# Turning the column order of the matrix passes in five of eight feed-forward stages

## The chip, the core and the metric

The kernel runs on one core of one Trainium2 chip. The metric is the time of one execution on the device in microseconds (us), the median of the runs shown. The core's engines appear in the profile as PE (TensorE, the matrix engine), PEld (its weight loads, which overlap PE), DVE (VectorE), ACT (ScalarE), POOL (GpSimd) and SP (SyncE, which only issues transfers here).

## The reference

Attention with a sigmoid in place of the softmax, and behind it two feed-forward blocks (the first with a squared ReLU, the second with a gate):

```
scores = scale * np.matmul(q, k.transpose(0, 1, 3, 2)) - np.log(S)
attn = 1.0 / (1.0 + np.exp(-scores))
x = np.matmul(attn, v)                        # 4 batches, 12 heads, S = 448, 64 wide
x = x.transpose(0, 2, 1, 3).reshape(1792, 768)
h = x @ w_in;  r = np.maximum(h, 0.0);  x = (r * r) @ w_out          # 768 -> 2048 -> 768
h = x @ w_in2; x = (h * (1.0 / (1.0 + np.exp(-1.702 * h)))) @ w_out2
```

All data is float32.

## The kernel before, in words

The kernel has two parts. The first, up to about 128 us, is the attention: scores (lines 293, 298, 317), a sigmoid on ACT, and the product with the values (lines 332, 346). The second holds the two feed-forward blocks, and it is the part that the change touches.

Each feed-forward block has two products (into the 2048-wide layer and out of it), and each is done for one half of the batches at a time, so there are eight stages (`STAGES`, line 49). A stage multiplies a matrix cut into 2 by 2 quarters, by a scheme with seven products in place of eight: sums and differences of quarters are prepared on DVE and ACT, and the seven are called P1 to P7. `ORDER` says in which order a stage issues them, in 56 *units* (7 products by 8 slices, `NF = 8`). A unit is three pairs of a weight tile of 128 by 128 and an operand of 448 columns (`S = 448`, one batch row).

Float32 accuracy comes from splitting each number into a rounded part and a remainder, both in the type float32r. `plan_weights` makes the weight tiles: a load `ld` from the scratch memory, then ACT writes the rounded part into `s` (line 459) and DVE the remainder (line 461). `Operand` (line 401) does the same for the moving operand `t`: its index 0 is the rounded part and its index 1 the remainder. `product` (line 464) then issues three *passes* of TensorE for each pair, all into the same 448 columns of one PSUM bank:

```
o = mem["ps"][:, b, :S]
nc.tensor.matmul(o, sh[:, cols], t[:, 0, k], start=start, stop=False, skip_group_check=True)
nc.tensor.matmul(o, sh[:, cols], t[:, 1, k], start=False, stop=False, skip_group_check=True)
nc.tensor.matmul(o, lo[:, cols], t[:, 0, k], start=False, stop=stop, skip_group_check=True)
```

These are lines 475, 476 and 477 of the profile. So a unit has 9 passes, a stage 504, and the eight stages 4032. Each pass has a weight load of its own in the trace (PEld), and reads its 448 columns from left to right, one run of consecutive float32 numbers in SBUF, and writes one run of consecutive numbers in PSUM. The results leave PSUM through ACT and DVE (lines 153, 156 and 635; 153 and 156 are helpers through which most of their work is recorded).

The order of all instructions on all engines is fixed when the program is built, by a planner (`settle` and `run`) that works with its own table of costs; `UNIT_US` is its cost of a unit and does not depend on how a unit walks its columns.

Of the kernel before, what the change touches and what calls it, by code (L numbers as in the profile page):

```python
# [16 lines left out]
B, H, S, D = 4, 12, 448, 64  # L17
# [15 lines left out]
UNITS = 7 * NF  # L33
# [44 lines left out]
WINDOW, URGENT = 0.25, 3.0  # L78

PACE = (6, 6, 5, 1, 4, 5, 5)  # L80


@with_exitstack
def sigmoid_attention_two_ffn(ctx: ExitStack, tc: tile.TileContext, qk, v, w, outT):
# [3 lines left out]
    nc = tc.nc  # L88
# [28 lines left out]
    mem = {"ps": ppool.tile([P, 8, 512], F32, name="ps")}  # L117
# [346 lines left out]
    def product(unit, pairs, ready):  # L464
        sl = SL[unit // 2 % NSLOT]

        def go():
            sh, lo = sl[:, 0, unit % 2], sl[:, 1, unit % 2]
            if unit == 0:
                one = [nc.const_aps.tensor(1.0, [P, n], mybir.dt.bfloat16) for n in (P, D)]  # L470
                nc.tensor.matmul(mem["ps"][:, pairs[0][0], :D], *one, start=True, stop=True)  # L471
            for b, c, t, k, start, stop in pairs:
                cols = slice(c * P, (c + 1) * P)
                o = mem["ps"][:, b, :S]
                nc.tensor.matmul(o, sh[:, cols], t[:, 0, k], start=start, stop=False, skip_group_check=True)  # L475
                nc.tensor.matmul(o, sh[:, cols], t[:, 1, k], start=False, stop=False, skip_group_check=True)  # L476
                nc.tensor.matmul(o, lo[:, cols], t[:, 0, k], start=False, stop=stop, skip_group_check=True)  # L477

        units[unit].fn = go
        units[unit].need(lows[unit // 2], ready)  # L480
        for b in {b for b, *_ in pairs}:
            units[unit].need(*held.pop(b, ()))
# [181 lines left out]
    def settle():  # L664
# [16 lines left out]
        assert len(order) == len(Node.all)  # L681
        marks = [(0, 0.0), (PACE[0], pe_at[units[0]])]
        for st, count in enumerate(PACE[1:]):
            marks.append((marks[-1][0] + count, pe_at[units[(st + 1) * UNITS]]))
# [184 lines left out]
```

## Time and profile before

| what | value |
|---|---|
| median of 3 runs | 951.23 us (950.59 to 951.44) |
| the profiled execution | 950.77 us, of which the span in the trace 949.0 us |
| granted TensorE clock over the span | 1.000 |
| busy: PE, PEld, DVE, ACT, POOL | 944.6, 822.8, 809.3, 604.6, 53.5 us |
| instructions of PE | 4949 matmuls, 4949 weight loads |
| passes of the eight stages | 3 lines of 1344 each |

The span runs from the first to the last instruction; the 1.8 us between it and the execution's own time lie outside. Busy time of PE is no measure by itself, since a matmul in the trace lasts longer than the distance to the next one (they are pipelined): where passes matter, the distance between their starts is to be read.

### The profile page before, as it was taken

Reading aid. Unit: us, or ns where it says so; the run is one execution under the profiler, and the core shown is the slowest. Engines: PE = TensorE matmul, PEld = TensorE weight load, DVE = VectorE, ACT = ScalarE, POOL = GpSimd, SP = SyncE. Lnnn points to the kernel's source line nnn. Section 1 sums busy time; section 2 is a strip of 40 time slices with the busy share of each in tenths; the row PEclk is TensorE's granted clock in tenths of the full one; section 3 lists DMA queues with packets and bytes.
Section 4 is the critical chain, followed back from the end, with each engine's and each line's share of the span. In section 5 each row is a group of like instructions: output and inputs, shape, how many; then the busy total and the mean of one; then the engine's idle time right before and its main releaser. Section 6 shows DMA issues by size and latency. Waiting matters only on the chain.

```text
span 949.0 us, 13696 instructions
## 1 busy us (share of the span) xinstructions
PE 944.6 (100%) x4949; PEld 822.8 (87%) x4949; DVE 809.3 (85%) x839; ACT 604.6 (64%) x715; POOL 53.5 (6%) x100
## 2 busy tenths in 40 slices
PE   9999999999999999999999999999999999999998
PEld 4555479999999999999999999999999999999997
DVE  3989986699877999999999987999989999778662
ACT  6788776778868775555464666657684646445551
POOL 0110100000000000000000000000000000000000
PEclk9999999999999999999999999999999999999999
DMA  8899989999886766896567699877975448754341
GB/s 340 301 335 356 335 293 332 324 354 334 290 324 227 250 231 212 317 364 216 161 243 286 202 359 325 312 247 251 351 279 171 133 146 288 261 166 132 115 137 58
DMA packets 98627, 245.75 MB, mean 259 GB/s; under 512 B 10752, under 2 KB 72960, under 8 KB 94464
## 3 DMA queue, kind: packets, MB, share of 16 engines
q1 hardware_dynamic: 84736, 150.51, 46.5%
q0 software_dynamic: 13824, 94.38, 27.2%
q8 instruction: 38, 0.62, 0.3%
q14 instruction: 29, 0.24, 0.1%
HBM read 175.11 MB, written 69.73 MB: 258 GB/s over the span
## 4 chain that ended last, share of the span: by engine, by line
PE 100%; ACT 0%; issue 0%
PE ps L475 29%; PE ps L476 29%; PE ps L477 29%; PE ps L332 6%; PE ps L298 5%; PE ps L346 1%; PE ps L317 1%; PE ps L790 0%; PE ps L293 0%; ACT xq L635 0%; PE ps L471 0%
## 5 line engine op out<-in xcount | busy, mean ns | idle before, releaser
L475 PE MATMUL ps<-t,s 128*128 128x448 f32 x1344 | 490.9, 365 | 0.0
L477 PE MATMUL ps<-t,s 128*128 128x448 f32 x1344 | 490.8, 365 | 0.0
L476 PE MATMUL ps<-t,s 128*128 128x448 f32 x1344 | 490.8, 365 | 0.0
L153 ACT ACTIVATE s<-ld 128x768 fp32r<-128x768 f32 x224 | 189.4, 846 | 249.4 <-PE ps L476 206.6
L477 PEld LDWEIGHTS ps<-t,s 128*128 128x128 f32 x1344 | 252.5, 188 | 19.9
L476 PEld LDWEIGHTS ps<-t,s 128*128 128x128 f32 x1344 | 252.5, 188 | 19.9
L475 PEld LDWEIGHTS ps<-t,s 128*128 128x128 f32 x1344 | 252.5, 188 | 19.9
L156 DVE TENSOR_TENSOR s<-ld,s 128x768 fp32r<-128x768 f32 x224 | 213.6, 954 | 61.7 <-ACT s L153 56.6
L156 DVE TENSOR_TENSOR t<-h,t 128x1344 fp32r<-128x1344 f32 (+1 forms) x72 | 100.4, 1397 | 8.8 <-ACT t L153 8.7
L153 ACT ACTIVATE t<-h 128x1344 fp32r<-128x1344 f32 (+1 forms) x72 | 85.6, 1190 | 4.4 <-DVE h L156 2.9
L153 ACT ACTIVATE h<-ps 128x448 f32<-128x448 f32 x112 | 59.8, 536 | 27.0 <-PE ps L477 26.8
L153 ACT ACTIVATE a<-ps,bias 128x896 f32<-128x896 f32 x72 | 66.1, 1023 | 3.2 <-PE ps L293 3.2
L332 PE MATMUL ps<-a,rv 128*64 128x448 f32 x288 | 56.8, 543 | 0.1
L217 DVE SCALAR_TENSOR_TENSOR dec<-raw,dec 128x1536 uint32<-128x1536 uint32 x32 | 56.2, 1755 | 0.5
L219 DVE SCALAR_TENSOR_TENSOR dec<-raw,dec 128x1536 uint32<-128x1536 uint32 x32 | 56.1, 1753 | 0.3
L153 ACT ACTIVATE dec<-raw 128x1536 f32<-128x1536 f32 x32 | 51.9, 1621 | 0.0
L156 DVE TENSOR_TENSOR h<-h,h 128x1344 f32<-128x1344 f32 (+1 forms) x36 | 50.0, 1397 | 1.0 <-DMA h<-hm 0.8
L153 ACT ACTIVATE h<-h 128x896 f32<-128x896 f32 x48 | 44.9, 945 | 4.8 <-DVE h L156 4.4
L332 PEld LDWEIGHTS ps<-a,rv 128*64 128x64 f32 x288 | 19.6, 137 | 32.4 <-issue 22.6
L213 DVE TENSOR_SCALAR dec<-dec 128x1536 f32<-128x1536 f32 x32 | 30.7, 959 | 15.6 <-ACT dec L153 15.6
L156 DVE TENSOR_TENSOR t<-xq,t 128x1344 fp32r<-128x1344 f32 x24 | 37.2, 1552 | 5.9 <-ACT t L153 5.4
L156 DVE TENSOR_TENSOR h<-ps,h 128x448 f32<-128x448 f32 x64 | 38.8, 619 | 2.8 <-PE ps L477 2.5
(58 smaller groups left out, 616.1 us busy)
## 6 DMA issues: line engine op xcount, KB each, us to landing
ld<-scr SPq DMA_DIRECT2D x448, 192.0 KB, 3.8
raw<-in_w POOLq DMA_DIRECT2D x32, 1536.0 KB, 8.2
scr<-dec POOLq DMA_DIRECT2D x32, 768.0 KB, 5.5
scr<-raw POOLq DMA_DIRECT2D x28, 576.0 KB, 6.2
hm<-h SPq DMA_DIRECT2D x32, 448.0 KB, 5.8
h<-hm SPq DMA_DIRECT2D x16, 672.0 KB, 5.4
rq<-in_qk SPq DMA_DIRECT2D x22, 448.0 KB, 8.2
rv<-in_v SPq DMA_DIRECT2D x12, 448.0 KB, 6.1
```

The lines of the kernel that those rows point to most:

```text
L153: nc.scalar.activation(out, in_, fn, **kw)
L156: nc.vector.tensor_tensor(out=out, in0=in0, in1=in1, op=op)
L213: dve(lambda: nc.vector.tensor_scalar(out=d, in0=d, scalar1=LEAST, scalar2=LARGEST, op0=ALU.max, op1=ALU.min), 4 * W, [dk], each=0.52e-3)
L217: dve(lambda: nc.vector.scalar_tensor_tensor(out=u, in0=raw[:, :, 0], scalar=29, in1=u, op0=ALU.logical_shift_right, op1=ALU.bitwise_or), ...
L219: dve(lambda: nc.vector.scalar_tensor_tensor(out=u, in0=raw[:, :, 1], scalar=0x80000000, in1=u, op0=ALU.bitwise_and, op1=ALU.bitwise_or), ...
L298: nc.tensor.matmul(ps[:, j, :S], kk[rows, keys], qq[rows, QUERIES], start=(i == 0), stop=(i == 2))
L317: nc.tensor.matmul(ps[out, j, :S], r[rows, :LEFT], r[rows, QUERIES], start=True, stop=True)
L332: nc.tensor.matmul(ps[rows, :S], t[:, hp % 2 * NFULL + c, rows], a[:, j], start=(c == 0), stop=False)
L346: nc.tensor.matmul(mem["ps"][out, b + i, :S], t[rows, 2 * NFULL, out], AL[rows, j], start=False, stop=True)
L475: nc.tensor.matmul(o, sh[:, cols], t[:, 0, k], start=start, stop=False, skip_group_check=True)
L476: nc.tensor.matmul(o, sh[:, cols], t[:, 1, k], start=False, stop=False, skip_group_check=True)
L477: nc.tensor.matmul(o, lo[:, cols], t[:, 0, k], start=False, stop=stop, skip_group_check=True)
```

## The change

Passes of a stage take their 448 columns in `PARTS` pieces of equal length: 1 piece in the first, fifth and eighth stage (as before), and 2, 7, 28, 56 and 112 pieces in the second, third, fourth, sixth and seventh. Within a piece the columns go from left to right as before; the pieces go from right to left. The operand read from SBUF and the output written to PSUM are walked in the same manner, so each column still arrives at the same place.

```diff
+PARTS = (1, 2, 7, 28, 1, 56, 112, 1)
...
+            parts = PARTS[unit // UNITS]
+
+            def turned(ap):
+                return ap.rearrange("p (a n) -> p a n", a=parts)[:, ::-1] if parts > 1 else ap
+
             for b, c, t, k, start, stop in pairs:
                 cols = slice(c * P, (c + 1) * P)
-                o = mem["ps"][:, b, :S]
-                nc.tensor.matmul(o, sh[:, cols], t[:, 0, k], start=start, stop=False, skip_group_check=True)
-                nc.tensor.matmul(o, sh[:, cols], t[:, 1, k], start=False, stop=False, skip_group_check=True)
-                nc.tensor.matmul(o, lo[:, cols], t[:, 0, k], start=False, stop=stop, skip_group_check=True)
+                o = turned(mem["ps"][:, b, :S])
+                hi, low = turned(t[:, 0, k]), turned(t[:, 1, k])
+                nc.tensor.matmul(o, sh[:, cols], hi, start=start, stop=False, skip_group_check=True)
+                nc.tensor.matmul(o, sh[:, cols], low, start=False, stop=False, skip_group_check=True)
+                nc.tensor.matmul(o, lo[:, cols], hi, start=False, stop=stop, skip_group_check=True)
```

No instruction is added, removed or moved on any engine. What changes in the built program is the shape of 2520 passes on PE. At the border of the sixth stage and the seventh its order of PE before reads (names are the tiles; the last column is partitions by columns):

```order
L477 MATMUL ps<-t_110,s_117 128x448
L475 MATMUL ps<-t_106,s_115 128x448
L476 MATMUL ps<-t_106,s_115 128x448
L477 MATMUL ps<-t_106,s_115 128x448
L475 MATMUL ps<-t_106,s_115 128x448
```

and with the change (lines 483 to 485 are the old 475 to 477):

```order
L485 MATMUL ps<-t_110,s_117 128x56x8
L483 MATMUL ps<-t_106,s_115 128x112x4
L484 MATMUL ps<-t_106,s_115 128x112x4
L485 MATMUL ps<-t_106,s_115 128x112x4
L483 MATMUL ps<-t_106,s_115 128x112x4
```

The same passes stand in the same places; 448 columns in one run have become 56 runs of 8 columns, and behind the border 112 runs of 4.

## Rows read from the trace of the kernel before

**Rows 1.** The page: busy time of each engine, and the chain that ended last.
```profile
PE 944.6 (100%) x4949; PEld 822.8 (87%) x4949; DVE 809.3 (85%) x839; ACT 604.6 (64%) x715; POOL 53.5 (6%) x100
...
PE 100%; ACT 0%; issue 0%
```

**Rows 2.** Waits of PE, whole span: who waited for whom, us, times, longest.
```profile
PE ps L790 <- PEq L858: 0.8, 1, 0.8
```

**Rows 3.** Busy time by stretch, one stage each: length, then engines, granted clock, DMA.
```profile
128.10:230.20 102.10, 102.10 (x505) 94.65 (x506) 83.62 (x92) 71.99 (x97) 8.75 (x16) 1.00 0.93 329
230.20:332.40 102.20, 102.20 (x506) 94.73 (x505) 86.39 (x97) 79.75 (x106) 8.70 (x16) 1.00 0.78 277
332.40:434.50 102.10, 102.10 (x505) 94.63 (x505) 99.28 (x93) 59.85 (x61) 3.74 (x7) 1.00 0.81 286
...
740.90:843.00 102.10, 102.10 (x506) 94.63 (x505) 91.82 (x82) 56.88 (x60) 0.00 (x0) 1.00 0.61 202
843.00:945.40 102.40, 102.40 (x506) 94.62 (x504) 60.39 (x54) 45.82 (x48) 0.00 (x0) 1.00 0.36 115
```

**Rows 4.** Timeline of PE, first and last passes: start, length, line, shapes.
```profile
128.34 0.37 PE L476 MATMUL ps<-t,s 128*128 128x448 f32 x1
128.54 0.36 PE L477 MATMUL ps<-t,s 128*128 128x448 f32 x1
128.74 0.37 PE L475 MATMUL ps<-t,s 128*128 128x448 f32 x1
...
945.09 0.37 PE L477 MATMUL ps<-t,s 128*128 128x448 f32 x1
```

**Rows 5.** Groups by line and shape, DVE: busy, mean ns, idle before.
```profile
L156 DVE TENSOR_TENSOR t<-h,t 128x1344 fp32r<-128x1344 f32 x48 | 74.6, 1554 | 8.8 <-ACT t L153 8.7
L217 DVE SCALAR_TENSOR_TENSOR dec<-raw,dec 128x1536 uint32<-128x1536 uint32 x32 | 56.2, 1755 | 0.5
L219 DVE SCALAR_TENSOR_TENSOR dec<-raw,dec 128x1536 uint32<-128x1536 uint32 x32 | 56.1, 1753 | 0.3
L156 DVE TENSOR_TENSOR t<-h,t 128x896 fp32r<-128x896 f32 x24 | 26.0, 1084 | 0.0
```

**Rows 6.** The same view, ACT.
```profile
L153 ACT ACTIVATE t<-h 128x1344 fp32r<-128x1344 f32 x48 | 63.1, 1315 | 2.2 <-PE ps L477 1.5 <-DVE h L156 0.7
L153 ACT ACTIVATE h<-ps 128x448 f32<-128x448 f32 x112 | 59.8, 536 | 27.0 <-PE ps L477 26.8
L153 ACT ACTIVATE dec<-raw 128x1536 f32<-128x1536 f32 x32 | 51.9, 1621 | 0.0
L153 ACT ACTIVATE t<-h 128x896 fp32r<-128x896 f32 x24 | 22.6, 940 | 2.2 <-DVE h L156 2.1
L153 ACT ACTIVATE xq<-ps 128x1344 f32<-128x1344 f32 x15 | 19.1, 1276 | 0.0
```

**Rows 7.** The chain that ended last, in order of time: start, length, what.
```profile
122.44 4.73 PE ps L332 x24
```

**Rows 8.** Groups by line and shape, PEld.
```profile
L475 PEld LDWEIGHTS ps<-t,s 128*128 128x128 f32 x1344 | 252.5, 188 | 19.9
```

## The prediction

> **What bounds the kernel now.** I read the page first: PE is busy for the whole span, and the chain of waits that ended last is PE alone [rows 1]. Busy time does not prove a bound, so the waits of PE came next: in 949.0 us TensorE waits for another engine once, for 0.8 us at the very start [rows 2]. So nothing in the eight stages is late for TensorE, and each nanosecond added to a pass shows in the end time in full. Then the stages: the stretches of one stage each are 102.1 to 102.4 us long, all with PE busy throughout at a granted clock of 1.00, although DVE's load in them goes from 60 to 99 us and the DMA share from 0.36 to 0.93 [rows 3]. A stage's length doesn't depend on what stands beside it. Last the distance between passes: from the start at 128.34 to that at 945.09 there are 4030 steps, (945.09 - 128.34) / 4030 = 202.67 ns each [rows 4]. A stage is 504 x 202.67 = 102.14 us, and the eight are 817.2 us of the span.
>
> **The change part by part.**
>
> *Instructions.* None is added, removed or moved; waits, transfers and the work of ACT, DVE, POOL and SP stay as they are. The cost of that is nothing, and needs no cover. As an output column gets its three passes (and the later ones of its sum) in one and the same order, a copy out of PSUM still waits for the last pass of its unit and no longer.
>
> *The walk.* What is new is that 2520 passes (5 stages of 504) jump within themselves. A pass in n pieces has n - 1 jumps, so the five stages have 1 + 6 + 27 + 55 + 111 = 200 for each of their 504 places: 100,800 jumps. Whatever a jump costs beyond the step to the next column is multiplied by this. The trace holds no matmul that jumps, so the price is bounded from its nearest rows.
>
> - From below: DVE reads the raw weights with every second word skipped (lines 217 and 219 read index 0 or 1 of pairs), one jump to each word. Its plain two-input operations take 1084 ns for 896 columns and 1554 ns for 1344, or 1.049 ns a column; continued to 1536 columns that makes 1755 ns. The skipping ones take 1755 and 1753 ns [rows 5]. The jump costs nothing there, and a price under nothing has no row behind it but the third rival's.
> - ACT reads the same pairs with the same skip. Its plain copies take 940 ns for 896 and 1315 ns for 1344 columns, 0.837 ns a column, so 1536 would be 1476 ns; the row says 1621 [rows 6]. At most 145 ns is due to 1536 jumps (it is another function too): 0.094 ns each, and 100,800 x 0.094 = 9.5 us here.
> - Reading PSUM: ACT takes 536 ns for one bank's 448 columns, and 1276 ns for three banks at once, two jumps [rows 6]. By 0.837 ns a column the second should be 536 + 896 x 0.837 = 1286 ns. Nothing for a jump of that kind.
> - From above: a jump might cost TensorE as much as one more column. A pass is 202.67 ns for 448 columns, 0.452 ns each [rows 4]; 100,800 x 0.452 = 45.6 us.
>
> I take nothing. The two skipping reads differ, and I choose DVE's because it is the harsher likeness with the cleaner comparison: there each word stands alone, while in the change four columns or more stand together, and even ACT's 0.094 ns is paid for single words. What I have no row for is TensorE's write into PSUM in pieces, and this is the weakest point of the sum. ACT's price and a column's price stay as ends for the range and the rivals.
>
> Of the SBUF side the Trainium skill, in "Vector Engine (DVE) Microarchitecture Reference", section "Measured stream behaviour on trn2", says that runs of two or more adjacent words on an even start stream at full rate and that the hops between them are free; that is of DVE, and the DVE rows here agree and go beyond it, since single words with a skip of one cost nothing either. By that rule the sum would be the same.
>
> *The sum.* Profiled execution 950.77 us (949.0 of span and 1.8 around it) + 0 for instructions + 100,800 x 0 for jumps = 950.8 us. The profiled execution lies 0.46 us under the median of 951.23, and the three runs lie within 0.85 us. What is forecast is the median, 951.2 us. About 0.2%, or 1.9 us, is what a measurement of this kernel can tell from no change; it is reached when a jump costs 1.9 us / 100,800 = 0.019 ns, a twenty-fourth of a column. So between "free" and "visible" there is almost no room, and the forecast is nearly a yes or no.
>
> **The rivals.**
>
> *A jump costs a small fixed time (slower).* Place: TensorE's reader or its PSUM writer, at each start of a piece, in the fourth, sixth and seventh stage above all (27, 55 and 111 jumps a pass). For it: 193 of the 200 jumps lie between pieces of 16 columns or fewer, and a pass that streams 448 columns in 202.67 ns asks for a word every 0.452 ns, more than twice as fast as DVE's 1.049 ns, so DVE's free skip may not carry over. Against it: nothing in the rows of SBUF or PSUM shows a price for groups of four words. It decides from 0.019 ns a jump on. At ACT's price the time is 951.2 + 9.5 = 960.7 us, with 0.05, 0.3, 1.3, 2.6 and 5.3 us in the five stages; at a column a jump it is 951.2 + 45.6 = 996.8 us, with 25.3 us of it in the seventh stage. A weight load of 188 ns stands beside each pass [rows 8]; if that set the beat and the columns had some nanoseconds to spare, the first jumps of a pass would be hidden and only the stages of 56 and 112 pieces would grow, which makes the time less but the sign no other. 8% for a price up to ACT's, 9% for one above it.
>
> *A pass in pieces falls to half its pace (much slower).* Place: the write into PSUM of every turned pass, whatever the number of pieces. For it: TensorE does have a pace about half as fast in this trace; the pairs of value products of line 332 take 4.73 us for 24, so 0.394 us a pair that runs at once, for the same 448 columns of plain float32 [rows 7]. Against it: all the pieces are of four columns or more, and the outputs of the attention are walked in one run, so no row shows it. The price is 2520 x (0.394 - 0.203) = 481 us, and the time 1432 us. The Trainium skill states such a rule, in "PSUM — Partial Sum Buffer", section "Specifications (TRN2)": PSUM has lines of 8 bytes, and any access pattern that isn't contiguous slows matmuls significantly. It gives no factor, and no run here shows it so far. Its page "Advanced Engine Details and Errata", section "PSUM Cachelines", adds that every two consecutive elements should be contiguous for best throughput, which all pieces here fulfil; by that reading the sum stays at 951.2 us. 5%.
>
> *The turned walk saves time (faster).* Each pass has 202.67 - 188 = 14.7 ns between the end of its weight load and the start of the next pass [rows 4, 8]. If a different first column let the next pass begin at once, the most is 2520 x 14.7 ns = 37 us, and 914 us. Against it: all passes of a stage begin at the same column as each other, before as after, so nothing in how one pass follows the other is new. 3%.
>
> That the change doesn't do what it says can be left out: the order of the changed program shows the pieces on all 2520 passes, and three stages stay as they were, which are controls within the same run.
>
> **How the numbers follow.** No visible change has 75%: the rows that resemble it (DVE's skip, ACT's jumps in PSUM) give nothing, and the missing row on PSUM writes keeps it from being more. Slower has 8 + 9 + 5 = 22%, faster 3%. The predicted time is that of the likeliest case, 951.2 us. Its own range is 0.2% either way, 949.3 to 953.1. To leave out no more than 2 in 10 the range reaches up to ACT's price, 961; the column's price, the half pace and the gain stay outside (17% together).
>
> **What the changed profile would show.** If right: the five stages stay at 102.1 us each and the distance of passes at 202.7 ns in all eight; waits of PE stay at 0.8 us; the rows of ACT and DVE are as before, as are DMA shares. If a jump has a price, the stages grow in proportion to 1, 6, 27, 55 and 111, and the first, fifth and eighth don't; the price is read from the seventh as (distance - 202.7) / 111. If the half pace is right, all five grow alike, the one with two pieces too. A growth only in the stages with the shortest pieces would speak for a limit on the length of a piece rather than a price of jumps. The prediction is wrong if the stage of 112 pieces alone is over 1.9 us longer, whatever the others do.

## The result, and the profile after

The changed kernel takes 958.54 us, the median of 4 runs (956.49 to 958.96), against 951.34 us (950.59 to 953.47, 4 runs) for the kernel before: a ratio of the means of 1.0068, 95% interval 1.0046 to 1.0089. That is slower, and clear of the runs' spread. The time lies inside the stated range, but on the side that had 22%, and not at the forecast of no visible change.

TensorE is the bound as before. The page and the waits of PE, which answer to [rows 1, 2]:

```profile
PE 952.7 (100%) x4949; PEld 823.0 (86%) x4949; DVE 810.0 (85%) x839; ACT 604.4 (63%) x715; POOL 52.6 (5%) x100
...
PE 100%; ACT 0%; issue 0%
```
```profile
PE ps L798 <- PEq L866: 0.8, 1, 0.8
```

No wait is new: still one, of 0.8 us. So the time must be in the distance of the passes. The timeline of PE, the first pass of each stage and the last pass of all (answers to [rows 4]; start, length, line, shapes):

```profile
128.67 0.45 PE L483 MATMUL ps<-t,s 128*128 128x448 f32 x1
...
230.89 0.36 PE L483 MATMUL ps<-t,s 128*128 128x448 f32 x1
...
333.70 0.36 PE L483 MATMUL ps<-t,s 128*128 128x448 f32 x1
...
437.85 0.37 PE L483 MATMUL ps<-t,s 128*128 128x448 f32 x1
...
540.88 0.36 PE L483 MATMUL ps<-t,s 128*128 128x448 f32 x1
...
643.03 0.37 PE L483 MATMUL ps<-t,s 128*128 128x448 f32 x1
...
747.18 0.37 PE L483 MATMUL ps<-t,s 128*128 128x448 f32 x1
...
851.34 0.36 PE L483 MATMUL ps<-t,s 128*128 128x448 f32 x1
...
953.28 0.37 PE L485 MATMUL ps<-t,s 128*128 128x448 f32 x1
```

The difference of two such starts, divided by 504, is the mean distance of a stage's passes (the last stage: by 503). All distances below are worked out so, with starts in ns.

| stage | pieces | distance before, ns | after, ns | longer, us (x 504) |
|---|---|---|---|---|
| 1st | 1 | 202.8 | 202.8 | 0.0 |
| 2nd | 2 | 202.7 | 204.0 | 0.7 |
| 3rd | 7 | 202.7 | 206.6 | 2.0 |
| 4th | 28 | 202.7 | 204.4 | 0.9 |
| 5th | 1 | 202.7 | 202.7 | 0.0 |
| 6th | 56 | 202.7 | 206.7 | 2.0 |
| 7th | 112 | 202.7 | 206.7 | 2.0 |
| 8th | 1 | 202.7 | 202.7 | 0.0 |

The seventh stage of the kernel before, from its first pass to the first of the eighth, for comparison with the last starts above (102.14 against 104.16 us):

```profile
741.00 0.36 PE L475 MATMUL ps<-t,s 128*128 128x448 f32 x1
...
843.14 0.37 PE L475 MATMUL ps<-t,s 128*128 128x448 f32 x1
```

The five make 7.6 us. The spans differ by 957.2 - 949.0 = 8.2 us; the other 0.6 lies before the first pass, which starts at 128.67 in place of 128.06, in a part that the change does not touch. The stages beside it, by stretch (answers to [rows 3]; length, then busy time and count of PE, PEld, DVE, ACT, POOL, granted clock, DMA share, GB/s):

```profile
333.70:437.85 104.15, 104.15 (x506) 94.61 (x505) 99.45 (x93) 59.89 (x62) 3.73 (x7) 1.00 0.81 281
437.85:540.88 103.03, 103.03 (x505) 94.71 (x504) 97.53 (x92) 56.64 (x56) 5.49 (x10) 1.00 0.61 206
540.88:643.03 102.15, 102.15 (x505) 94.65 (x504) 91.13 (x102) 66.69 (x88) 7.61 (x14) 1.00 0.87 308
...
747.18:851.34 104.16, 104.16 (x505) 94.69 (x504) 92.00 (x81) 56.95 (x61) 0.00 (x0) 1.00 0.60 198
```

The clock is full in all of them, and the two stages shown of about 104.15 us have a DMA share of 0.81 and 0.60 and a DVE load of 99 and 92 us: the extra follows neither. It follows the walk, but in no order of the number of jumps (27 jumps cost less than half of what 6 do).

### The profile page after: what moved, and what is told of

Read it like the earlier page. It is cut to its first block, busy times and chain, and to the rows that moved or that the text cites. A ratio compares the mean times of both kernels' runs of the same rounds, so it can differ in the third digit from the quotient of the medians.

```text
span 957.2 us, 13696 instructions
## 1 busy us (share of the span) xinstructions
PE 952.7 (100%) x4949; PEld 823.0 (86%) x4949; DVE 810.0 (85%) x839; ACT 604.4 (63%) x715; POOL 52.6 (5%) x100
## 4 chain that ended last, share of the span: by engine, by line
PE 100%; ACT 0%; issue 0%
PE ps L485 29%; PE ps L484 29%; PE ps L483 29%; PE ps L334 6%; PE ps L300 5%; PE ps L348 1%; PE ps L319 1%; PE ps L798 0%; PE ps L295 0%; ACT xq L643 0%; PE ps L473 0%
## 5 line engine op out<-in xcount | busy, mean ns | idle before, releaser
L219 DVE SCALAR_TENSOR_TENSOR dec<-raw,dec 128x1536 uint32<-128x1536 uint32 x32 | 56.1, 1754 | 0.5
L221 DVE SCALAR_TENSOR_TENSOR dec<-raw,dec 128x1536 uint32<-128x1536 uint32 x32 | 56.1, 1754 | 0.3
```

What stands on the lines that cost most here:

```text
L219: dve(lambda: nc.vector.scalar_tensor_tensor(out=u, in0=raw[:, :, 0], scalar=29, in1=u, op0=ALU.logical_shift_right, op1=ALU.bitwise_or), ...
L221: dve(lambda: nc.vector.scalar_tensor_tensor(out=u, in0=raw[:, :, 1], scalar=0x80000000, in1=u, op0=ALU.bitwise_and, op1=ALU.bitwise_or), ...
```

## The experiments

A run here is one profiled execution, unless it says more. All of them have the same passes in the same order; only what a pass reads, loads or writes differs, and in two runs the place of the buffers. Where the columns or weights are not those of the kernel before, the products of the changed stages are other numbers, as each expectation says.

**Which side pays.** The first run turns the read alone, the second the write alone.

```diff
+READ = (1, 2, 7, 28, 1, 56, 112, 1)      # second run: all 1
+WRITE = (1, 1, 1, 1, 1, 1, 1, 1)         # second run: (1, 2, 7, 28, 1, 56, 112, 1)
-                o = turned(mem["ps"][:, b, :S])
-                hi, low = turned(t[:, 0, k]), turned(t[:, 1, k])
+                o = turned(mem["ps"][:, b, :S], wr)
+                hi, low = turned(t[:, 0, k], rd), turned(t[:, 1, k], rd)
```

> Only the operand read from SBUF is taken in pieces from right to left (2, 7, 28, 56, 112 as in the change); PSUM is written from left to right, so the columns of those stages come out permuted. Distance of passes in the changed kernel: 204.0, 206.6, 204.4, 206.7, 206.7 ns in the five stages, 202.7 in the others. Theory R (the reader of the moving operand pays, the writer doesn't): the same five distances. Theory W (the PSUM writer pays): 202.7 ns in all eight stages, time as before, 951 us. Both sides pay: something between, under 206.

> Only the output in PSUM is walked in pieces from right to left; the operand is read from left to right, so the columns of those stages come out permuted. Theory R: 202.7 ns in all eight stages, 951 us. Theory W: 204.0, 206.6, 204.4, 206.7, 206.7 ns as in the changed kernel, 958.5 us.

Read alone: 204.0, 206.6, 204.4, 206.7, 206.7 ns in the five stages, 961.0 us. Write alone: 202.7 ns in all eight, 951.17 us, against 951.28 us for the kernel before beside it. The seventh stage of both, from its first pass to the first of the eighth; read alone:

```profile
747.31 0.37 PE L486 MATMUL ps<-t,s 128*128 128x448 f32 x1
...
851.47 0.36 PE L486 MATMUL ps<-t,s 128*128 128x448 f32 x1
```

and write alone:

```profile
741.40 0.37 PE L486 MATMUL ps<-t,s 128*128 128x448 f32 x1
...
843.55 0.36 PE L486 MATMUL ps<-t,s 128*128 128x448 f32 x1
```

104.16 against 102.15 us. The whole cost is the reader's. The write into PSUM in 2 to 112 pieces, right to left, is free; the rule of the Trainium skill in "PSUM — Partial Sum Buffer", "Specifications (TRN2)", that any access pattern that isn't contiguous slows matmuls significantly, doesn't hold for these pieces.

**Ends or jumps.** Two walks with other ends and other counts.

```diff
+                return ap.rearrange("p (a b n) -> p b a n", a=parts // 2, b=2)   # evens, then odds: 4, 8, 28, 56, 112, 224 pieces
```
```diff
+READ = (1, 4, 14, 16, 8, 224, 448, 1)
+WRITE = (1, 4, 14, 16, 8, 224, 448, 1)                                           # right to left
```

> Pieces as many and as short as in the change, on both sides, but first all even pieces from left to right, then all odd ones: 4, 8, 28, 56, 112 and 224 pieces in the second, third, fourth, fifth, sixth and seventh stage. A pass begins at column 0 and ends at column 447 as before. Theory E (a pass pays once, for where it begins and ends against its neighbours, not for jumps): 202.7 ns in the stages of 4 to 112 pieces. Theory J (jumps or the form of the pattern pay, up to 4 ns a pass hidden or capped): 204 to 207 ns in them. For 224 pieces of two columns neither says more than that it may be higher.

> The change with other counts from right to left on both sides: 4, 14, 16, 8, 224 and 448 pieces in the second to seventh stage. Theory E: 4, 14, 16 and 8 pieces all lie between 202.7 and 206.7 ns, in no order of their counts, and 224 pieces of two columns as well. Theory J: they rise with the count, 4 below 8 below 14 below 16. A third idea, that single columns break a pair in PSUM or a line in SBUF, would show in 448 pieces alone, as a distance well over 210 ns, up to twice.

Evens then odds: 206.7 ns for 4 pieces and for 8, 213.3 for 28, 204.2 for 56, 203.3 for 112, and 395.5 for 224 pieces of two columns. Right to left: 205.0 for 4 pieces, 204.0 for 14, 206.7 for 16, 204.4 for 8, and 206.7 for both 224 pairs and 448 single columns. Both theories fall. The second kernel alone would have spoken for E (no order of counts, all between 204.0 and 206.7), but E fails because in the first a walk from column 0 to 447 costs up to 10.7 ns when it jumps on the way; J fails because 112 pieces cost less than 28, and 448 no more than 7. The third idea fails for single columns, which cost no more than the pieces. The 395.5 ns are something else. The timeline of the evens-then-odds run, the first passes of the fourth stage (28 pieces) and the fifth, then of the seventh (224) and the eighth:

```profile
438.98 0.37 PE L485 MATMUL ps<-t,s 128*128 128x448 f32 x1
...
546.50 0.37 PE L485 MATMUL ps<-t,s 128*128 128x448 f32 x1
...
751.88 0.56 PE L485 MATMUL ps<-t,s 128*128 128x448 f32 x1
...
951.22 0.39 PE L485 MATMUL ps<-t,s 128*128 128x448 f32 x1
```

The seventh takes 199.3 us. There a pass takes 8 bytes, skips 8 and comes back for those later, so each 16 bytes are visited twice; right to left, pairs and single columns of the same 16 bytes follow each other, and that costs nothing of the kind. This run walks both sides so, and only the walk from right to left was tried on the write alone; whether the reader or the writer pays the 395.5 ns is therefore not shown.

**The place against the weights.** A theory B was formed: the reads of the moving operand meet those of the weight load that runs beside each pass (188 ns, [rows 8]), and their relative place and order decide how often. Against it stood S: the extra belongs to the read's own pattern. The read begins late by some columns:

```diff
+OFF = (0, 4, 8, 16, 32, 48, 2, 0)
+                at = (i * NK + k) * S + OFF[st] - (64 if OFF[st] and i * NK + k == 2 * NK - 1 else 0)
+                return turned(t.rearrange("p i k n -> p (i k n)")[:, at : at + S], READ[st])   # READ: 1 in all stages
```

> All passes read one run from left to right, but the run begins 4, 8, 16, 32, 48 and 2 columns late in the second to seventh stage (so the products of those stages are of shifted columns); weights and PSUM as before. Theory B (the reads of the moving operand clash in SBUF with the weight load that runs beside each pass, so their relative place sets the extra): the distance differs between the offsets, anywhere from 200 to 207 ns. Theory S (the reader's own start or pattern, no weights in it): 202.7 ns at each offset of whole 16 bytes (4 to 48), at most a little more at 2.

202.2 ns 4 columns late, 206.6 at 8, 200.0 at 16, 204.0 at 32, 202.2 at 48, 206.4 at 2. (The last row of a buffer begins 64 columns earlier, so that the read stays inside it.) S falls: with its place alone, a read in one run, from left to right, differs by up to 6.6 ns, and by 4.0 ns between the two places, 16 and 32 late, whose distances came back in the next run. The best is under the kernel before. Starts of the first and second stage, then of the fourth (16 late) and fifth:

```profile
128.35 0.45 PE L487 MATMUL ps<-t,s 128*128 128x448 f32 x1
...
232.58 0.36 PE L487 MATMUL ps<-t,s 128*128 128x448 f32 x1
...
438.65 0.36 PE L487 MATMUL ps<-t,s 128*128 128x448 f32 x1
...
539.45 0.36 PE L487 MATMUL ps<-t,s 128*128 128x448 f32 x1
```

The lower pair is that stage, 100.80 us. The upper pair is the first stage, not late at all and with the same instructions and addresses as before: 104.23 us, 206.8 ns. That was not expected by either theory, and I come back to it below. It also means that a distance near 206.7 which was seen only once (8 and 2 late here) can't be told from such a stage.

Moving the weight tile in place of the operand tells whether the operand's own address counts:

```diff
+OFF = (0, 4, 8, 16, 32, 48, 48, 0)       # weights late; the seventh stage also reads 7 pieces right to left
+                at = (2 * h + unit % 2) * W + c * P + OFF[st] - (64 if OFF[st] and h and unit % 2 and c == NK - 1 else 0)
+                return flat[:, at : at + P]              # flat = sl.rearrange("p h u n -> p (h u n)")
```

> The moving operand stays where it is and is read in one run; the weight tile begins 4, 8, 16, 32, 48 columns late in the second to sixth stage, and in the seventh 48 late with the operand in 7 pieces right to left (products of other weights). Theory B with a period of 64 columns (weights late by n are the operand late by 64 - n): 16 late gives the 202.2 of the operand 48 late, 32 gives 204.0, 48 gives 200.0, and 7 pieces with 48 give 200.0 too; 4 and 8 differ from 202.7. If only the operand's own address counts: 202.7 in all the stages read in one run and 206.6 in the seventh.

206.7 ns at 4, 204.4 at 8, 202.2 at 16, 204.0 at 32, 200.0 at 48, and 200.0 for the 7 pieces at 48. The weights 16, 32 and 48 late give what the operand gave 48, 32 and 16 late, as theory B with a period of 64 columns (256 bytes) says; for 4 late no operand 60 late was run. Timeline of the sixth and seventh stage (starts of the sixth, the seventh and the eighth):

```profile
643.14 0.36 PE L490 MATMUL ps<-t,s 128*128 128x448 f32 x1
...
743.95 0.36 PE L490 MATMUL ps<-t,s 128*128 128x448 f32 x1
...
844.75 0.37 PE L490 MATMUL ps<-t,s 128*128 128x448 f32 x1
```

100.8 us each, one run and 7 pieces alike: at this place the 7 pieces that cost 2.0 us in the change cost nothing. The operand has not moved here and its distances change, while above the weights had not moved: the relative place of operand and weight tile is what counts.

**Less weight, and weights spread out.** Two runs change the weight load.

```diff
+WIDE = (128, 64, 64, 64, 32, 32, 32, 128)                    # read: one run, 7 pieces, singles; twice
+                cols = slice(c * P, c * P + WIDE[st])
+                o = mem["ps"][: WIDE[st], b, :S]
```
```diff
+STEP = (1, 2, 3, 2, 3, 2, 3, 1)                              # read: one run twice, 7 pieces twice, singles twice
+                cols = slice(c, c + STEP[st] * (P - 1) + 1, STEP[st]) if STEP[st] > 1 else slice(c * P, (c + 1) * P)
```

> Weight tiles of 64 columns (second to fourth stage) or 32 (fifth to seventh), so half or a quarter of the rows of each product is computed; read straight, in 7 pieces right to left, and in single columns right to left, in that order for each width. Theory B: with less weight to load beside a pass the extra of the turned walk shrinks from 4.0 ns to 2 or less at 64 columns and 1 or less at 32, and the straight distance falls under 202.7. Theory S: turned minus straight stays 4.0 ns at both widths.

> The weight tile takes each second (second, fourth and sixth stage) or each third column (third, fifth, seventh), so its load touches two or three times the memory; the moving operand is read in one run in the second and third stage, in 7 pieces right to left in the fourth and fifth, in single columns right to left in the sixth and seventh (the products are of other weights). Theory B: the distances change with the step, for straight and turned reads: over 202.7 for one run, off 206.7 for the turned. Theory S: 202.7 for one run and 206.7 for both turned walks, at any step, unless the load itself gets longer than a pass, which its row would show (over 188 ns).

With 64 weight columns, and with 32 likewise: 202.2 ns for one run, 202.2 for 7 pieces, 204.4 for single columns. First passes of the three stages with 64, and of the next:

```profile
229.74 0.37 PE L486 MATMUL ps<-t,s 128*64 128x448 f32 x1
...
331.67 0.36 PE L486 MATMUL ps<-t,s 128*64 128x448 f32 x1
...
433.59 0.37 PE L486 MATMUL ps<-t,s 128*64 128x448 f32 x1
...
536.62 0.37 PE L486 MATMUL ps<-t,s 128*32 128x448 f32 x1
```

The loads got shorter, by the groups of PEld of that run:

```profile
L486 PEld LDWEIGHTS ps<-t,s 128*64 128x64 f32 x504 | 67.9, 135 | 35.9
...
L486 PEld LDWEIGHTS ps<-t,s 128*128 128x128 f32 x336 | 63.1, 188 | 5.0
...
L486 PEld LDWEIGHTS ps<-t,s 128*32 128x32 f32 x504 | 54.3, 108 | 47.3
```

The extra of the 7 pieces is gone and that of single columns is 2.2 ns in place of 4.0, which speaks for B. But 32 columns give no less than 64, so the extra isn't in proportion to the load; for single columns B's "2 or less" missed by little and its "1 or less" clearly. What keeps those 2.2 ns isn't shown. Spread weights: at a step of 2 one run and 7 pieces both have 203.7 ns, at a step of 3 both 204.4, and single columns 205.9 and 210.0. So with another weight walk (whose start moved too, by at most two columns) the 7 pieces lose their extra over the one run, as B says. The loads at a step of 3 are longer than a pass (0.25 us each in the timeline), so I read no more from that run.

**Lines of 16 bytes.** Turned reads that begin late, on and off whole 16 bytes:

```diff
+READ = (1, 112, 112, 56, 7, 7, 28, 1)
+OFF = (0, 2, 4, 2, 16, 8, 4, 0)
```

> Turned reads that also begin late: 112 pieces 2 columns late, 112 pieces 4 late, 56 pieces 2 late, 7 pieces 16 late, 7 pieces 8 late, 28 pieces 4 late, in the second to seventh stage (shifted columns in the products); PSUM straight. Both theories, of the 16-byte line: 112 pieces of 4 columns that lie across two lines each read every line twice, so the distance goes far up, towards 390 ns; 56 pieces of 8 across three lines make about half of that extra, 300 ns. On whole lines: Theory B has distances that change with the offset (7 pieces: other than 206.6; 28 pieces: other than 204.4), Theory S leaves 206.7, 206.6, 206.6 and 204.4 ns.

112 pieces 2 columns late and 56 pieces 2 late: 326.6 ns both, where one was to be 390 and the other 300. On whole 16 bytes: 112 pieces 4 late 206.7, 7 pieces 16 late 200.0, 7 pieces 8 late 206.7, 28 pieces 4 late 206.7. The stage of 112 pieces across lines, from its first pass to the next stage's, then the stage of 56 pieces likewise:

```profile
230.05 0.49 PE L487 MATMUL ps<-t,s 128*128 128x448 f32 x1
...
394.68 0.39 PE L487 MATMUL ps<-t,s 128*128 128x448 f32 x1
...
498.86 0.49 PE L487 MATMUL ps<-t,s 128*128 128x448 f32 x1
...
663.49 0.38 PE L487 MATMUL ps<-t,s 128*128 128x448 f32 x1
```

164.6 us each, in place of 102.1. PSUM is written straight here, so this is the reader's. It is shown that turned pieces of four and eight columns pay when they begin two columns off whole 16 bytes. Beginning off is not dear by itself: one run 2 columns late took 206.4 ns, and pairs and single columns from right to left 206.7. Nor does the price follow the number of visits: the 112 pieces make 224 visits to a line in a pass and the 56 pieces 168, at one price. So its size was misjudged, and stays unexplained. For B, the 7 pieces again follow the place (200.0, and 206.6 in the change); the 28 pieces changed too (206.7, and 204.4).

**Is there a place where the fine walk is free?**

```diff
+READ = (1, 112, 1, 112, 1, 112, 1, 112)
+OFF = (12, 8, 24, 32, 40, 48, 56, 40)     # second run: READ all 448, OFF = (4, 8, 16, 24, 32, 40, 48, 56)
```

> Other places of the moving operand against the weight tile, in one kernel: one run beginning 12, 24, 40 and 56 columns late in the first, third, fifth and seventh stage; 112 pieces right to left, 8, 32, 48 and 40 columns late in the second, fourth, sixth and eighth (products of shifted columns, PSUM straight). Theory B: the one-run distances lie between 200.0 and 206.7 ns and differ by place, none under 200.0 unless the place at 16 is not the best; for the 112 pieces, whose order runs as the weights' (right to left), the place decides as well, so at least one of the four should come out under 206.7. If all four stay at 206.7, the fine walk pays whatever the place, and place matters for walks from left to right alone.

> All stages read single columns from right to left, beginning 4, 8, 16, 24, 32, 40, 48 and 56 columns late (shifted columns, PSUM straight). Theory B: a walk from right to left in single columns visits the same lines in the same order as the 112 pieces, so at 8, 32, 40 and 48 it has their 204.4, 206.7, 204.4 and 204.4 ns. If no place gives under 204 ns, a walk against the weights' place costs at least 1.8 ns over the one run of before whatever the place; if one gives 200 to 203 ns, the fine walk is free at that place.

One run: 203.1 ns at 12, 205.3 at 24, 200.0 at 40, 204.4 at 56 (the weights 8 late had given the same 204.4). 112 pieces: 204.4 at 8, 206.7 at 32, 204.4 at 48 and 40. Single columns: 206.8 at 4, 204.4 at 8, 206.7 at 16, 24 and 32, 204.4 at 40, 48 and 56. The second stage of the singles (8 late), from its first pass to the next stage's, is 103.03 us:

```profile
232.65 0.37 PE L487 MATMUL ps<-t,s 128*128 128x448 f32 x1
...
335.68 0.37 PE L487 MATMUL ps<-t,s 128*128 128x448 f32 x1
```

Where both were measured, 112 pieces and single columns agree: at 8, 32, 40 and 48 here, and at 0 and 4 in the runs above, to 0.2 ns. So the order in which the 16-byte lines come is what counts, not the order within a line; and of the nine places tried for a fine walk (0 with them) none is under 204.4 ns. One run from left to right ranges from 200.0 to 206.6. At the place that the kernel has, 202.7, it stood below all of them, and so the change could only lose on the fine walks. Elsewhere the sign can turn: 8 columns late, the one run had 206.6 ns and both fine walks 204.4 (the 206.6 was seen once).

**A faster version.** The place that gave 200.0 ns can be had for all stages, with the reads in one run: weight tiles allocated first, then 64 unused bytes, then the operands. One pad serves all passes because, by their shapes, the buffers, operand rows (1792 bytes) and weight tiles (512 bytes) are whole multiples of 256 bytes.

```diff
-    T = [cpool.tile([P, 2, NK, S], F32R, name=f"t{n}") for n in range(NT)]
     LD = [cpool.tile([P, 2, W], F32, name=f"ld{n}") for n in range(NLOAD)]
     SL = [cpool.tile([P, 2, 2, W], F32R, name=f"s{n}") for n in range(NSLOT)]
+    cpool.tile([P, 16], F32, name="pad")
+    T = [cpool.tile([P, 2, NK, S], F32R, name=f"t{n}") for n in range(NT)]
```

> The kernel before (all reads in one run), with the buffers of the moving operand put 64 bytes further against the weight tiles in SBUF: the weight tiles are allocated first, then 16 unused columns, then the operands. Theory B (place of the moving operand against the weight tile): 200.0 ns in all eight stages, as the read that began 16 columns late; 4032 x 2.67 = 10.8 us less, 940.5 us, faster than both kernels. Theory S (own pattern of the read): 202.7 ns and 951 us. If the 200.0 ns came from the absolute address, the same gain is possible, so the run with the weights moved has to tell these apart.

> The change as it is (1, 2, 7, 28, 1, 56, 112, 1 pieces, both sides), with the same 64 bytes between weight tiles and operands. Theory B: other distances than 204.0, 206.6, 204.4, 206.7, 206.7; the 7 pieces at 200.0 as in the run with offsets, the one-run stages at 200.0. Theory S: the old five, and 202.7 in the others.

The kernel before with this layout takes 941.0 us (940.6 to 941.05, 4 runs) against 951.68 us (951.0 to 952.27, 7 runs): a ratio of the means of 0.9887, interval 0.987 to 0.9903, and faster than both kernels. The first passes of its first three stages, and the last pass:

```profile
127.83 0.45 PE L476 MATMUL ps<-t,s 128*128 128x448 f32 x1
...
228.73 0.36 PE L476 MATMUL ps<-t,s 128*128 128x448 f32 x1
...
329.53 0.36 PE L476 MATMUL ps<-t,s 128*128 128x448 f32 x1
...
934.12 0.37 PE L478 MATMUL ps<-t,s 128*128 128x448 f32 x1
```

From 228.73 on, a stage is 100.80 us: 200.0 ns a pass in all seven, and 200.2 in the first. The gain by the passes is 4032 x 2.67 ns = 10.8 us; by the medians it is 10.7.

The change with the same layout takes 951.98 us in one run: 202.2 ns with 2 pieces, 200.0 with 7, 206.7 with 28, 56 and 112, 200.0 in the later two stages of one run and 200.2 in the first. For 56 and 112 pieces nothing changed, where B had other distances. The 7 pieces have become free by moving a buffer, while the fine walks have not.

**The same kernel twice more.**

> The kernel before, unchanged, profiled once more. If place and order fix the distance alone, all eight stages are at 202.7 ns as in its first profile. If weight loads and moving reads can lock into more than one rhythm at the same addresses (206.7 ns was seen in one untouched stage of two runs with offsets), one or more stages stand at 206.7, and the time is 2.0 us more for each.

> The same once more, for the same question: 202.7 ns in all stages, 951 us; or some at 206.7, with 2.0 us more for each, up to 967 us for all eight.

202.7 ns in all stages of both (202.8 in the first), 951.09 and 951.53 us. So the second distance at unchanged addresses did not come back in these two, and what was seen of it stands in the last section.

## Why the prediction was wrong

*What bounds the kernel:* right. TensorE's pace set the end, no other engine hid or added anything, and the sum of the stages' growth (7.6 us) is the span's but for 0.6. But "a stage's length doesn't depend on what stands beside it" was read from stages in which DVE's load and the DMA share differ [rows 3]; the weight load is the same beside every pass, so these rows couldn't show its part.

*Instructions cost nothing:* right; waits are the same. The skipping rows of DVE are at 1754 ns each, within 1 ns of before [rows 5]:

```profile
L219 DVE SCALAR_TENSOR_TENSOR dec<-raw,dec 128x1536 uint32<-128x1536 uint32 x32 | 56.1, 1754 | 0.5
L221 DVE SCALAR_TENSOR_TENSOR dec<-raw,dec 128x1536 uint32<-128x1536 uint32 x32 | 56.1, 1754 | 0.3
```

The weight loads too have the mean that they had [rows 8], by the groups of PEld:

```profile
L483 PEld LDWEIGHTS ps<-t,s 128*128 128x128 f32 x1344 | 252.5, 188 | 22.6
```

*The walk costs 100,800 x 0:* wrong, and this is the step that failed. It took the price of a jump, nothing, from the likeness of DVE's skip, and multiplied by the number of jumps. Neither holds. What the runs showed in its place is a price per pass and on the read alone: up to 4.0 ns in the change, in no proportion to the number of jumps, given by the order in which the pass goes through its 16-byte lines and by where they lie against the weight tile. A row of DVE has no weight load running beside it. For the 7 pieces the load is shown to be the partner: moving only the weights, or narrowing them, took their extra away. For the fine walks that holds in part: they stayed at 204.4 ns or more at every place, and with a narrow load at 2.2 ns over the one run, and the cause of this rest stays open. As measured, the five stages cost 504 x (1.3 + 4.0 + 1.8 + 4.0 + 4.0) ns = 7.6 us; the prediction's rows could not have given these prices.

*The weakest point named, PSUM:* it was no weak point. The write in pieces cost 0.0 ns a pass.

*The rivals.* A fixed price per jump fell: 0.7, 2.0, 0.9, 2.0, 2.0 us were measured in the five stages where ACT's price gave 0.05, 0.3, 1.3, 2.6, 5.3. That its total of 9.5 us comes near the 7.2 between the medians is chance; the range held the time for the wrong reason. The half pace fell with the result itself (958.54, not 1432 us) and with the run that turned the write alone. The turned walk that saves time did not occur in any of the five stages; but of the 14.7 ns that it named, 2.67 ns a pass can be had, by place and not by walk.

*The signs to look for.* "The stage of 112 pieces alone over 1.9 us longer" came true (2.0 us). The controls worked: the three stages of one run stayed at 202.7 ns, and this is what made the five legible in one profile.

## What to carry to other kernels

Where passes follow each other without a gap, the place of the moving operand against the weight tile in SBUF is worth a try before any reordering: here 64 unused bytes gave 1.1%, and the distances fit a period of 256 bytes. Walks in pieces from right to left are free on the PSUM side down to four columns, and on the SBUF side they cost at most 2% of a pass against the one run at this kernel's place, as long as each 16-byte line is finished before the next (5% was the most for such lines in another order, 28 pieces evens then odds on both sides). Turned pieces of four or eight columns that begin off a line paid 60% more, and a walk in pairs that skips every second pair on both sides took nearly double. A cost that is read from another engine's rows leaves out what runs beside it on this one.

## What the runs showed of the hardware that was not expected

- A read of float32 columns that leaves a 16-byte line and comes back to it can be dear: 326.6 ns for turned pieces across lines, and 206.7 for pairs or single columns taken right to left, which finish each line first. The 395.5 ns of pairs that skip a pair fit this, but there the write skipped too. "SBUF — State Buffer" of the Trainium skill, in "Specifications (TRN2)", asks for two hits a line for full bandwidth; the 112 pieces across lines had two columns of a line in each visit and took 61% more than one run.
- Operand and weight tile influence each other's pace by their relative place: 200.0 to 206.6 ns for one and the same walk. That the two reads contend in the memory itself is a guess that fits these, but what inside SBUF or TensorE does it was not tried and stays open. Against a plain form of it stand two results: a load shorter than 64 columns took no more of the extra away, and the 56 and 112 pieces kept 206.7 ns in the new layout.
- The same instructions at the same addresses can settle at two distances. Untouched stages stood at 206.8 ns (the first of the run with late reads) and 206.7 ns (the last of the run with late weights), and at 202.7 in three profiles of the kernel before. A stage that settles so costs 504 x 4.0 ns = 2.0 us, and one of the kernel's four times beside the result, 953.47 us, lies 2.0 to 2.9 us over the other three. In the changed kernel 956.49 us lies 2.0 to 2.5 us under the other three, as if one stage had settled lower; neither time has a profile of its own. One further run of the kernel before, beside the first of the two sweeps, took 968.5 us, which all eight stages at 206.7 would come near (16.1 us more); it left no profile. What decides it stays open.
